# An attention and gated feed-forward kernel: a later value load, an output weight loaded in two parts, one half's attention placed earlier, and one more Strassen pair

## The chip, the core and the metric

The kernel runs on one core of one Trainium2 chip. The metric is the device time of one execution in microseconds (us). The kernel before takes 239.68 us, the median of three runs (239.47 to 240.16).

The engines are named as the profile names them: PE multiplies matrices (PEld loads its stationary operand), DVE works elementwise on tensors, ACT does activations and copies, POOL does simple elementwise work and issues some DMAs, SP issues DMAs. Each engine runs its own instructions in the order in which the program emits them.

## The reference

Four batches of eight heads, 768 positions, 64 channels a head. Each position attends to the 95 before it, itself, and eight global positions; a bias falls off linearly with distance. The result, as 3072 tokens of 512 channels, goes through a gated feed-forward with 1536 hidden channels:

```python
scores = scale * q @ k.T + bias            # kept where global or local, else -1e9
a = exp(scores - max); a = a / a.sum()
x = (a @ v), heads side by side            # 3072 x 512
out = (maximum(x @ w_gate, 0) * (x @ w_val)) @ w_out
```

## The kernel before, in words

The 3072 tokens are eight halves of 384, two to a batch, numbered 0 to 7 in the code; "the third half" is number 2. A half has three tiles of 128 tokens. Its work is: load q and k (`load_qk`, SP's queue) and v (`load_v_half`, POOL's queue); eight casts to bf16 on POOL (`piece_cast`); three DMA transposes on SP's queue (`piece_x`), which make queries and keys with the channels on partitions (tile `kqT`); copies that order the keys for the windows (`piece_order`, tile `kT`, two head pairs on POOL and, for the third half, two on ACT); attention of four pairs of heads; and the feed-forward.

Attention of a half is a list, `attention_pieces`: for each pair of heads three pieces `QK` (the scores in four PSUM banks, their exponentials on ACT, the masks on DVE), two pieces `AV` (the product with v on PE in one bank each, logarithm and inverse on ACT) and a norm `N` on DVE, which writes `xT`, the feed-forward's input. Scores and value products take turns in five banks `x`. Two gaps, of empty pieces, make up the list: with one piece in each it has 26 places, with two in each, as for the third half, 28.

The feed-forward of a half, `ffn_pieces`, is a list of pieces of four to eight matmuls, each with the weight 0.65: 24 that make gate and value for the twelve blocks of 128 hidden channels (`f1`: ReLU on ACT, product on DVE into tile `ht`), and then the output product (`f2`). A plain output tile is four pieces `outp` of three 512-column matmuls. A pair of tiles can instead go through Strassen's scheme (Winograd's form, `winograd`): seven products of six matmuls with 256 columns, four sums of hidden tiles (`add`, line 535, on DVE) and sums of the output weight (`wo_sum`, line 835, on DVE, made once). Each half multiplies its first two tiles this way, but for half 0; `PAIRED` names the halves whose third tile forms a pair with the next half's third tile (`sums3`, `add3`). Products of gate, value and output take turns in three banks `ff`, the Strassen products also in banks `x`.

The order of the work is written by hand. `weave` emits a list of feed-forward pieces one after the other and puts other pieces in between: an extra with position p is emitted as soon as the weights emitted so far reach p times the sum of the weights. `spread` gives a list of pieces evenly spaced positions. So PE's order is this order, and so is that of every engine for what is emitted through it. What is emitted outside runs at once as far as its engine and its data allow.

Around the change the order is this. Halves 0 and 1 have their attention at the start, the first weights arrive, and POOL issues the third groups of w_gate and w_val and then all of w_out (`wo_sb`, `loads`, line 798). POOL then fills the second v buffer with ones, issues the third half's v loads (line 841), makes seven casts, copies one element of `wo_sb` (tile `held`, line 845, which waits until w_out is there), and makes the eighth cast; SP issues the three transposes; POOL orders the keys of two pairs. Then `load_qk_after(3, nc.gpsimd)` lets POOL write one element of each staging tile, which stands ahead of SP's loads of the fourth half's q and k, and POOL issues that half's v. Three weaves follow; the third (lines 852 to 856) holds the last blocks of halves 0 and 1, their output products, the third half's attention and the fourth half's casts and transposes. The halves after that come from a loop (line 859).

Of the kernel before, what the change touches and what calls it, by code (L numbers as in the profile page):

```python
# [15 lines left out]
def kernel(  # L16
# [12 lines left out]
    nc = tc.nc  # L29
# [4 lines left out]
    DM = H * D  # L34
    DFF = moe_w_gate.shape[1]
    N_DC = DM // 128
    N_FC = DFF // 128
    HP = H // 2
    QH = S // 2
    NN = 3  # L40
# [55 lines left out]
    wo_sb = const.tile([128, N_FC, DM], BF16)  # L96
# [3 lines left out]
    def w_of(t, dc, fc):  # L100
        f = fc % GW
        return t[fc // GW][:, dc, f * 128 : (f + 1) * 128]
# [15 lines left out]
    def v_dst(b, r0, r1, j):  # L118
        t = vbuf[b % 2][r0:r1, j, D:]
        return t.rearrange("p (h z) -> p h z", z=2 * D)[:, :, 0:D]  # L120

    def load_v_globals(b):
        nc.gpsimd.dma_start(out=v_dst(b, 0, NG, 0),
                            in_=v[b, :, 0:NG, :].rearrange("h p d -> p h d"))

    def spread_v_globals(b, j0=1, j1=NT):
        if b == 0:
            for j in range(j0, j1):
                nc.sync.dma_start(out=v_dst(b, 0, NG, j), in_=v_dst(b, 0, NG, 0))
        else:  # L130
            t = vbuf[b % 2]
            nc.sync.dma_start(out=t[0:NG, j0:j1, :], in_=t[0:NG, 0:1, :].to_broadcast(
                [NG, j1 - j0, (2 * H + 1) * D]))

    def load_v(b, j, r0=0, r1=KT):
        n = min(r1, S - KT * j) - r0
        nc.gpsimd.dma_start(  # L137
            out=v_dst(b, NG + r0, NG + r0 + n, j),
            in_=v[b, :, KT * j + r0 : KT * j + r0 + n, :].rearrange("h p d -> p h d"))
# [5 lines left out]
    def load_v_half(s):  # L145
        b, half = divmod(s, 2)
        if half == 0:
            load_v_globals(b)
            if s != 2:
                spread_v_globals(b)  # L150
        for j in range(4) if half == 0 else range(4, NT):
            load_v(b, j)

    def load_w(dst, src, f0, f1):
        nc.gpsimd.dma_start(out=dst, in_=src[:, f0:f1].rearrange("(c p) f -> p c f", p=128))

    def load_w_group(i):
        load_w(wg[i], moe_w_gate, i * GW * 128, (i + 1) * GW * 128)
# [218 lines left out]
    def early_pieces(s):  # L377
        out = [(0.0, lambda p=p, i=i: piece_cast(s, p, i)) for i in range(2) for p in range(HP)]
        out += [(0.0, lambda n=n: piece_x(s, n)) for n in range(NN)]
        out += [(0.0, lambda p=p: piece_order(s, p)) for p in range(HP)]  # L380
        return out
# [111 lines left out]
    def attention_pieces(s):  # L493
        QK = lambda p: [(0.15, lambda g=g: piece_qk(s, p, g)) for g in range(3)]
        AV = lambda p: [(0.29, lambda e=e: piece_av(s, p, e)) for e in range(2)]
        N = lambda p: [(0.0, lambda: piece_norm(s, p))]
        g = QK(3)
        a = AV(2)
        gap = [(0.0, lambda: None)] * (2 if s == 2 else 1)
        return (QK(0) + QK(1) + AV(0) + N(0) + gap + QK(2) + AV(1) + N(1) + gap  # L500
                + g[0:1] + a[0:1] + g[1:2] + a[1:2] + g[2:3] + N(2) + AV(3) + N(3))

# [89 lines left out]
        return add, [(0.65, (m1, m2, m3, m4, m5, m6, m7)[i - 1]) for i in order]  # L592


    PAIRED = (4, 6)
    third_of = {}

    def ffn_pieces(c):
        ht = ht_pool.tile([128, N_FC, QH], BF16, name="ht")
        st = {}  # L600

        def product(w, key, fc, d0, d1):
            key = key, fc
            if d0 == 0 and key not in st:
                st[key] = psum["ff"].tile([128, 512], FP32, name="ff_ps")
            for dc in range(d0, d1):
                nc.tensor.matmul(st[key][:, 0:QH], lhsT=w_of(w, dc, fc), rhs=xT_of[c][:, dc, :],  # L607
                                 start=(dc == 0), stop=(dc == N_DC - 1))

        def gate(fc, d0=0):  # L610
            product(wg, "g", fc, d0, N_DC)
            psg = st["g", fc]
            gr = gr_pool.tile([128, QH], BF16, name="grelu")
            nc.scalar.activation(gr, psg[:, 0:QH], AF.Relu, bias=0.0, scale=1.0)  # L614
            st["gr", fc] = gr

        def val(fc, d0=0):
            product(wv, "v", fc, d0, N_DC)
            psv = st["v", fc]
            nc.vector.tensor_tensor(ht[:, fc, :], psv[:, 0:QH], st["gr", fc], op=ALU.mult)  # L620

        def outp(n, part):
            if part == 0:
                st["o"] = psum["ff"].tile([128, 512], FP32, name="ff_ps")
            ps2 = st["o"]
            for fc in range(part * N_FC // 4, (part + 1) * N_FC // 4):
                nc.tensor.matmul(ps2, lhsT=ht[:, fc, n * 128 : (n + 1) * 128],  # L627
                                 rhs=wo_sb[:, fc, :],
                                 start=(fc == 0), stop=(fc == N_FC - 1))
            if part == 3:  # L630
                osb = late["osb"].tile([128, DM], FP32, name="osb")
                nc.scalar.copy(osb, ps2)
                nc.sync.dma_start(out=out_v[c, n], in_=osb)

        def begin():
            two = psum["s"].tile([128, 2, 512], FP32, name="s_ps")
            st["g", 1], st["v", 1] = two[:, 0], two[:, 1]
            for d0, d1 in ((0, 2), (2, N_DC - 1)):
                for key, w in (("g", wg), ("v", wv)):
                    for fc in range(2):  # L640
                        product(w, key, fc, d0, d1)

        plain = range(NN) if c < 1 else () if c - c % 2 in PAIRED else (NN - 1,)
        add, products = winograd([(c, ht, 0), (c, ht, 1)], "sums", (1, 5, 6, 4, 7, 2, 3) if c == NHALF - 1 else
                                 (1, 2, 5, 6, 4, 3, 7) if c in PAIRED else (1, 5, 4, 6, 2, 3, 7))
        behind = {2: [lambda: add(3, 0, 3)], 7 if c == 2 else 5: [lambda: add(3, 3, 6)], 8: [lambda: add(1, 0, 3)],
                  9: [lambda: add(2, 0, 3)], 10: [lambda: add(4, 0, 3)]}
        rest = tuple(lambda j=j: add(j, 3, 6) for j in (1, 2, 4))
        if c in PAIRED:
            third_of[c] = ht  # L650
        elif c - 1 in PAIRED:
            add3, products3 = winograd([(c, ht, NN - 1), (c - 1, third_of[c - 1], NN - 1)], "sums3",
                                       (1, 5, 4, 6, 2, 3, 7))
            behind.update({1: [lambda: add3(1)], 6: [lambda: add3(2)], 7: [lambda: add3(3)]})
            rest = (lambda: add3(4),) + rest

        def val_and_sums(fc):
            val(fc)
            for f in behind.get(fc, ()):
                f()  # L660

        begin_of[c] = (begin, lambda fc=0: gate(fc, N_DC - 1), lambda fc=0: val(fc, N_DC - 1))
        f1 = []
        for fc in range(N_FC):
            f1.append((0.65, lambda fc=fc: gate(fc)))
            f1.append((0.65, lambda fc=fc: (val if c < 1 else val_and_sums)(fc)))
        f2 = [(0.65, lambda n=n, part=part: outp(n, part))
              for n in plain for part in range(4)]
        if c >= 1:
            f2 += (products3 if c - 1 in PAIRED else []) + products  # L670
            places = (2, 3, 5) if plain else (0, 1, 2) if c in PAIRED else (0, 1, 2, 3)
            for at, f in list(zip(places, rest))[::-1]:
                f2.insert(at, (0.0, f))
        return f1, f2


    def spread(items, first, last):

        n = len(items)
        return [(first + (i + 0.5) / n * (last - first), f) for i, (_, f) in enumerate(items)]  # L680
# [102 lines left out]
    f1_0, f2_0 = ffn_pieces(0)  # L783
# [13 lines left out]

    def loads():
        load_w_group(2)
        load_w(wo_sb, moe_w_out, 0, DM)  # L800
        Z()

    more = {"K0": lambda: load_qk_after(2), "S20": loads}
# [1 line left out]
    for f in ("m0 g0 g1 v0 m3 K3 m2 g2 m1 v1 K2 v2 S30 K0 S31 K1 S21 g3 S20 v3 S01 A3 N3 S00 S11 "  # L805
              "g6 g7 A2 S10 g4 v7 A0 N2 v4 v6 A1 N0 N1 g5 v5").split():
        i = int(f[1])
# [30 lines left out]
    nc.gpsimd.memset(vbuf[1][:, NT - 1, :].bitcast(mybir.dt.uint32), 0)  # L838
    for j in range(NT):
        fill_ones(nc.gpsimd, 1, j)  # L840
    load_v_half(2)
    E = [f for _, f in early_pieces(2)]
    casts, xs, order_k = E[0:8], E[8:11], E[11:15]
    held = rc_pool.tile([1, 1], BF16, name="held")
    for f in (*casts[:7], lambda: nc.gpsimd.tensor_copy(held, wo_sb[0:1, N_FC - 1, 0:1]),
              casts[7], *xs, lambda: spread_v_globals(1), *order_k[:2]):
        f()
    load_qk_after(3, nc.gpsimd)
    load_v_half(3)
    weave(f1_1[G[0]])  # L850
    weave(f1_1[G[1]], [(0.1 + 0.12 * j, lambda j=j: fill_ones(nc.vector, 0, j)) for j in range(NT)])
    weave(f1_0[G[2]] + f1_1[G[2]] + f2_0 + f2_1,
          [(0.33, order_k[2]), (0.38, order_k[3])],
          spread(attention_pieces(2), 0.375, 0.925), spread(early_pieces(3), 0.58, 0.88),
          spread([(0.0, lambda j=j, part=part: wo_sum(j, part)) for j in (1, 3, 2, 4) for part in range(2)],
                 0.1, 0.74))

    ahead = {}
    for c in range(2, NHALF):
# [53 lines left out]
```

## Time and profile before

| | us |
|---|---|
| median of three runs | 239.68 |
| lowest and highest | 239.47, 240.16 |
| the profiled execution | 240.08 |
| its span, first to last instruction | 238.3 |
| PE busy in the span | 231.7 |
| DVE, ACT, POOL busy | 171.8, 156.1, 89.5 |

The profile is of one execution. Its page gives busy times, the chain of work that ended last, and groups of equal instructions by line; the trace answers for stretches of time. A matmul's end is modelled and lies some 0.16 us past the start of the next one where they are dense, so PE's pace is read from start to start. TensorE's clock was granted in full from the first matmul to the last. The DMA engines move 132 GB/s in the mean; 47176 of 70515 packets are under 512 B. The third weave runs from about 46.3 to 76.2 us.

The page's lines on DMA issues (out<-in, issuing engine, count, KB each, median us from issue to landing) that bear on the change:

```profile
vbuf<-in_v_dram POOLq DMA_DIRECT2D x21, 120.0 KB, 7.7
wo_sb<-in_moe_w_out_dram POOLq DMA_DIRECT2D x1, 1536.0 KB, 19.0
```

### The profile page before, as it was taken

How to read it: one execution, taken by the hardware profiler on the slowest of the kernel's cores; microseconds unless marked ns; L12 is line 12 of the kernel's file. 1: busy time of each engine (PE TensorE's matmuls, PEld its weight loads, DVE VectorE, ACT ScalarE, POOL GpSimd, SP SyncE). 2: the span in 40 equal slices, each digit the busy share in tenths (PEclk: the TensorE clock that was granted, in tenths of full speed). 3: DMA queues.
4: the chain of work that ended last, by engine and by line, in shares of the span. 5: the costliest groups of instructions: out<-in, count | busy, mean ns of one | idle time of the engine just before them, and what ended most of it. 6: DMA issues, size and time to landing. Idle time of an engine off the chain costs nothing.

```text
span 238.3 us, 5431 instructions
## 1 busy us (share of the span) xinstructions
PE 231.7 (97%) x1977; PEld 150.1 (63%) x1981; DVE 171.8 (72%) x456; ACT 156.1 (66%) x358; POOL 89.5 (38%) x204
## 2 busy tenths in 40 slices
PE   7899999999999999999999999999999999999994
PEld 3655565655557566666667666856588666766683
DVE  7775965768756778666787677868985786955752
ACT  5896983438767777757777678557686578634330
POOL 6795897007433860903275042723350000000000
PEclk9999999999999999999999999999999999999999
DMA  6999999993996897098519955198432200020022
GB/s 208 183 170 174 241 263 213 191 162 47 286 205 124 260 194 135 10 183 259 101 33 111 236 155 111 25 157 249 78 59 88 90 1 0 4 88 0 3 80 97
DMA packets 70515, 31.42 MB, mean 132 GB/s; under 512 B 47176, under 2 KB 67400, under 8 KB 70488
## 3 DMA queue, kind: packets, MB, share of 16 engines
q0 software_dynamic: 32800, 8.71, 36.0%
q1 hardware_dynamic: 36472, 21.45, 34.3%
q10 hardware_dynamic: 1216, 0.92, 1.2%
q8 instruction: 15, 0.25, 0.4%
q14 instruction: 12, 0.10, 0.1%
HBM read 28.41 MB, written 6.29 MB: 146 GB/s over the span
## 4 chain that ended last, share of the span: by engine, by line
PE 86%; DMA 7%; DVE 2%; POOL 1%; ACT 1%; issue 1%; DVEq 0%
PE ff_ps L607 50%; PE ff_ps L549 12%; DMA wg<-in_moe_w_gate_dram 7%; PE ff_ps L627 7%; PE x_ps L427 6%; PE x_ps L549 5%; PE x_ps L397 4%; PE t_ps L700 1%; PE t_ps L459 1%; POOL kq L737 1%; PE t_ps L272 1%; DVE es L359 0%; DVE ht L620 0%; ACT lnd L436 0%; DVE osb L574 0%
## 5 line engine op out<-in xcount | busy, mean ns | idle before, releaser
L607 PE MATMUL ff_ps<-xT,wg 128*128 128x384 bf16 x380 | 77.7, 326 | 0.4 <-DMA wg<-in_moe_w_gate_dram 0.2
L607 PE MATMUL ff_ps<-xT,wv 128*128 128x384 bf16 x380 | 77.6, 326 | 0.2 <-DVE osb L574 0.2
L614 ACT ACTIVATE grelu<-ff_ps 128x384 bf16<-128x384 f32 x95 | 46.5, 491 | 45.1 <-PE ff_ps L607 23.2
L620 DVE TENSOR_TENSOR ht<-ff_ps,grelu 128x384 bf16<-128x384 f32 x95 | 52.7, 555 | 30.2 <-PE ff_ps L607 19.1
L607 PEld LDWEIGHTS <-wg 128*128 128x128 bf16 x384 | 36.1, 98 | 23.6 <-issue 1.0
L607 PEld LDWEIGHTS <-wv 128*128 128x128 bf16 x384 | 35.8, 98 | 23.3 <-issue 0.5
L406 ACT ACTIVATE es<-x_ps 128x360 bf16<-128x360 f32 (+2 forms) x96 | 35.6, 447 | 3.2 <-PE x_ps L397 3.2
L359 DVE TENSOR_TENSOR es<-es,m_all 128x432 bf16<-128x432 bf16 (+4 forms) x108 | 29.7, 325 | 6.0 <-ACT es L406 5.8
L446 DVE TENSOR_TENSOR xT<-x_ps,rcp 64x384 bf16<-64x384 f32 x48 | 26.6, 554 | 9.2 <-ACT rcp L441 8.4
L436 ACT ACTIVATE lnd<-x_ps 64x384 f32<-64x384 f32 x48 | 23.3, 485 | 10.9 <-PE x_ps L427 10.2
L363 POOL CAST kqc<-ks 128x384 bf16<-128x384 f32 x24 | 12.1, 554 | 31.7 <-DMA ks<-in_k_dram 31.7
L549 PEld LDWEIGHTS <-s 128*128 128x128 bf16 x216 | 21.1, 98 | 2.9 <-issue 0.4
L549 PE MATMUL ff_ps<-t,s 128*128 128x256 bf16 x162 | 21.6, 272 | 0.3 <-ACT osb L584 0.3
L427 PE MATMUL x_ps<-es,vbuf 128*128 128x216 bf16 (+4 forms) x216 | 21.8, 225 | 0.0
L137 POOL DMA_DIRECT2D vbuf<-in_v_dram x25 | 21.6, 881 | 0.3 <-DVE s L535 0.3
L427 PEld LDWEIGHTS <-vbuf 128*128 128x128 bf16 x216 | 15.8, 97 | 6.8
L627 PE MATMUL ff_ps<-wo_sb,ht 128*128 128x512 bf16 x68 | 17.6, 379 | 0.2
L549 PEld LDWEIGHTS <-ht 128*128 128x128 bf16 x162 | 15.5, 98 | 2.3
L263 POOL COPY kT<-kqT 128x240 bf16<-128x240 bf16 x16 | 7.1, 442 | 22.2 <-DMA kqT<-kqc 19.2
L363 POOL CAST kqc<-qs 128x384 bf16<-128x384 f32 x24 | 12.1, 541 | 6.2 <-DMA qs<-in_q_dram 6.2
L535 DVE TENSOR_TENSOR s<-ht 128x384 bf16<-128x384 bf16 (+1 forms) x32 | 12.5, 392 | 0.8
L441 ACT ACTIVATE rcp<-lnd 128x384 f32<-128x384 f32 x24 | 12.6, 524 | 0.8
(118 smaller groups left out, 247.0 us busy)
## 6 DMA issues: line engine op xcount, KB each, us to landing
out_dram<-osb SPq DMA_DIRECT2D x23, 256.0 KB, 2.4
ks<-in_k_dram SPq DMA_DIRECT2D x6, 768.0 KB, 6.2
qs<-in_q_dram SPq DMA_DIRECT2D x6, 768.0 KB, 11.5
vbuf<-in_v_dram POOLq DMA_DIRECT2D x21, 120.0 KB, 7.7
wo_sb<-in_moe_w_out_dram POOLq DMA_DIRECT2D x1, 1536.0 KB, 19.0
wg<-in_moe_w_gate_dram POOLq DMA_DIRECT2D x2, 512.0 KB, 9.8
wv<-in_moe_w_val_dram POOLq DMA_DIRECT2D x2, 512.0 KB, 11.0
wg<-in_moe_w_gate_dram POOLq DMA_DIRECT2D x2, 256.0 KB, 5.8
```

Of the source, the lines that this page charges most:

```text
L137: nc.gpsimd.dma_start(out=v_dst(b, NG + r0, NG + r0 + n, j), in_=v[b, :, KT * j + r0 : KT * j + r0 + n, :].rearrange("h p d -> p h d"))
L359: nc.vector.tensor_mul(for_all, for_all, mk)
L363: nc.gpsimd.tensor_copy(kqc[:, :, i].rearrange("t n (h d) -> t h n d", d=D)[:, 2 * p : 2 * p + 2], of[s][:, 2 * p : 2 * p + 2, :].rearrang ...
L406: nc.scalar.activation(es[:, e, 0:c], banks[e][:, 0:c], AF.Exp, bias=0.0, scale=scale)
L427: nc.tensor.matmul(av3[:, :, a : a + w], lhsT=vb[:, j, z0 : z0 + 128], rhs=es[:, e, c : c + NN * w].rearrange("k (n p) -> k n p", n=NN), s ...
L436: nc.scalar.activation(ln[o0 : o0 + 64], av[d0 : d0 + 64, 0:QH], AF.Ln, bias=0.0, scale=1.0)
L446: nc.vector.tensor_tensor(xT_of[s][r, p, :], av_of[s, p, e][r, 0:QH], av_of[s, p, "r"][r], op=ALU.mult)
L549: nc.tensor.matmul(st[key][:, 0:D2], lhsT=left(i), rhs=right(i), start=start and i == 0, stop=i == N2 - 1, skip_group_check=not start)
L607: nc.tensor.matmul(st[key][:, 0:QH], lhsT=w_of(w, dc, fc), rhs=xT_of[c][:, dc, :], start=(dc == 0), stop=(dc == N_DC - 1))
L614: nc.scalar.activation(gr, psg[:, 0:QH], AF.Relu, bias=0.0, scale=1.0)
L620: nc.vector.tensor_tensor(ht[:, fc, :], psv[:, 0:QH], st["gr", fc], op=ALU.mult)
L627: nc.tensor.matmul(ps2, lhsT=ht[:, fc, n * 128 : (n + 1) * 128], rhs=wo_sb[:, fc, :], start=(fc == 0), stop=(fc == N_FC - 1))
```

## The change

Four things are changed.

1. `PAIRED` becomes (0, 4, 6): the third tiles of halves 0 and 1 become a Strassen pair. Half 0 multiplies two tiles plainly, half 1 none. The pair's four sums stand between the pieces of half 0's plain tiles. For the later pairs, two of the four sums are made in two parts each, at more places (`behind`).
2. The third half's v loads are issued after its eight casts and three transposes. The `held` copy no longer stands before the eighth cast.
3. w_out is loaded in two parts, blocks 0 to 7 where it was loaded, and blocks 8 to 11 behind the key order of the third half's first two pairs. The `held` copy, which waits for the second part, comes behind that.
4. In the third weave, the third half's attention is spread over 0.18 to 0.88 instead of 0.375 to 0.925, with one gap at a time instead of two. ACT's key orders stand at 0.18 and 0.22 instead of 0.33 and 0.38, the sums of w_out at 0.34 to 0.63 instead of 0.1 to 0.74.

```diff
+    def load_wo(i0, i1):
+        nc.gpsimd.dma_start(out=wo_sb[:, i0:i1], in_=moe_w_out[i0 * 128 : i1 * 128].rearrange("(c p) f -> p c f", p=128))
...
-        gap = [(0.0, lambda: None)] * (2 if s == 2 else 1)
+        gap = [(0.0, lambda: None)]
...
-    PAIRED = (4, 6)
+    PAIRED = (0, 4, 6)
...
-        plain = range(NN) if c < 1 else () if c - c % 2 in PAIRED else (NN - 1,)
+        plain = range(2) if c < 1 else () if c - c % 2 in PAIRED else (NN - 1,)
...
-            behind.update({1: [lambda: add3(1)], 6: [lambda: add3(2)], 7: [lambda: add3(3)]})
-            rest = (lambda: add3(4),) + rest
+            if c > 1:
+                behind[1] = [lambda: add3(1)]
+                for fc, j, i in ((3, 2, 0), (4, 3, 0), (6, 2, 3), (7, 3, 3)):
+                    behind[fc] = [lambda j=j, i=i: add3(j, i, i + 3)]
+                rest = (lambda: add3(4),) + rest
+            else:
+                for j in range(1, 5):
+                    f2_0.insert(2 * j - 1, (0.0, lambda j=j: add3(j)))
...
-            places = (2, 3, 5) if plain else (0, 1, 2) if c in PAIRED else (0, 1, 2, 3)
+            places = (2, 3, 5) if plain else (0, 1, 2) if c in PAIRED or c == 1 else (0, 1, 2, 3)
...
-        load_w(wo_sb, moe_w_out, 0, DM)
+        load_wo(0, 8)
...
-    load_v_half(2)
...
-    for f in (*casts[:7], lambda: nc.gpsimd.tensor_copy(held, wo_sb[0:1, N_FC - 1, 0:1]),
-              casts[7], *xs, lambda: spread_v_globals(1), *order_k[:2]):
+    for f in (*casts, *xs, lambda: load_v_half(2), lambda: spread_v_globals(1), *order_k[:2],
+              lambda: load_wo(8, N_FC), lambda: nc.gpsimd.tensor_copy(held, wo_sb[0:1, N_FC - 1, 0:1])):
...
-          [(0.33, order_k[2]), (0.38, order_k[3])],
-          spread(attention_pieces(2), 0.375, 0.925), spread(early_pieces(3), 0.58, 0.88),
+          [(0.18, order_k[2]), (0.22, order_k[3])],
+          spread(attention_pieces(2), 0.18, 0.88), spread(early_pieces(3), 0.58, 0.88),
...
-                 0.1, 0.74))
+                 0.34, 0.63))
```

More of the change, by code (lines that the diff above doesn't have):

```diff
@@ L641, in begin @@
                         product(w, key, fc, d0, d1)
-        plain = range(NN) if c < 1 else () if c - c % 2 in PAIRED else (NN - 1,)
+        plain = range(2) if c < 1 else () if c - c % 2 in PAIRED else (NN - 1,)
         add, products = winograd([(c, ht, 0), (c, ht, 1)], "sums", (1, 5, 6, 4, 7, 2, 3) if c == NHALF - 1 else
-                                 (1, 2, 5, 6, 4, 3, 7) if c in PAIRED else (1, 5, 4, 6, 2, 3, 7))
+                                 (1, 2, 5, 6, 4, 3, 7) if c in PAIRED else (1, 5, 4, 6, 2, 3, 7)) if c else ((), ())
         behind = {2: [lambda: add(3, 0, 3)], 7 if c == 2 else 5: [lambda: add(3, 3, 6)], 8: [lambda: add(1, 0, 3)],
```

## Prediction

> **What bounds the kernel now.** I read the page first, then the chain of waits in order of time, then the timelines of PE, POOL and SP around the third half's queries and keys, then busy time by stretch. The page, its span and its busy shares:
>
> ```profile
> span 238.3 us, 5431 instructions
> ...
> PE 231.7 (97%) x1977; PEld 150.1 (63%) x1981; DVE 171.8 (72%) x456; ACT 156.1 (66%) x358; POOL 89.5 (38%) x204
> ...
> PE 86%; DMA 7%; DVE 2%; POOL 1%; ACT 1%; issue 1%; DVEq 0%
> ```
>
> PE sets the time: 86% of the chain is PE, and the 7% of DMA is the wait for the first weights, before 27.7 us, which the change does not touch. So an edit is worth the PE time it removes, or a stall of PE that it removes or makes. Modelled ends of matmuls run past the next start, so I count from start to start. From 34.5 us on PE stops visibly in three places only. The chain in order of time shows them (start, us, what):
>
> ```profile
> 61.58 1.94 PE ff_ps L627 x9
> ...
> 74.77 0.53 ACT rcp L441
> ...
> 75.91 0.56 DVE xT L446
> 76.50 0.42 DVE osb L569
> 76.92 0.34 DVE osb L574
> 77.31 1.47 PE ff_ps L607 x8
> ...
> 169.74 0.48 DVE ht L620
> 170.26 2.11 PE ff_ps L607 x12
> ...
> 225.57 1.31 PE ff_ps L549 x12
> ```
>
> Stops one and two come at the end of the stage in which the third half's attention is woven (call it G2): its last logarithms and inverse hold ACT, so a Strassen copy comes late (product 7 starts at 75.60, its predecessor's six matmuls of 0.109 were through at 75.18: 0.42 us); its last norms hold DVE at 75.33 to 76.47, so a sum frees its bank late (77.31 where 76.25 + 4 x 0.1636 = 76.90: 0.41 us). The third, 0.34 us before 170.26, is in the sixth half: DVE is late with a product of gate and value. Rows 61.58 and 225.57 give the price of a matmul: 1.94/9 = 0.2157 us for 512 columns, 1.31/12 = 0.1093 us for 256.
>
> **The work itself.** Two third tiles as plain products were 24 matmuls of 512 columns, 24 x 0.2157 = 5.18 us. As a pair they are 7 x 6 = 42 of 256, 42 x 0.1093 = 4.59 us. **-0.6 us.** The evacuation changes from two ACT copies of 580 ns to four of 370 ns, plus four DVE operations of 420 ns and four sums (L535, 128x768) of 546 to 627 ns: 4 us more on DVE, where it hides only if DVE has room (below).
>
> **The stalls removed.** The third half's 26 attention pieces now end at 0.88 of 38 items instead of 0.925 of 39 (an item is one piece of the weave, 0.65 in its own unit, 0.655 us on PE): last norm behind item 33, 5 items ahead of the end instead of 3. ACT and DVE are then through before the last products. I count both stops as gone: **-0.8 us**. Halving the third-tile sums of halves six and eight takes 0.3 us of DVE (0.71 at 167.52 becomes about 0.37) from in front of the late multiply: **-0.3 us**. It reappears two pieces earlier, in DVE gaps of 0.8 and 0.4 us. Sum of the gains: 1.7 us.
>
> **What comes forward.** The first scores of the third half ran at 56.76, behind item 16. At 0.1935 x 38 = 7.4 they now come behind item 8: 56.76 - 8 x 0.655 = 51.52 us. What they need is in the timelines of POOL and of SP (start, us, what, in brackets the idle time before it and what ended it):
>
> ```profile
> 40.10 1.53 POOL L363 CAST kqc<-qs 128x384 bf16<-128x384 f32 x3 [1.56 <-DMA qs<-in_q_dram]
> 47.47 0.18 POOL L845 COPY held<-wo_sb 1x1 bf16<-1x1 bf16 x1 [5.83 <-DMA wo_sb<-in_moe_w_out_dram]
> ...
> 54.92 0.63 POOL L259 COPY kT<-kqT 128x360 bf16<-128x360 bf16 x1 [6.83 <-DMA kqT<-kqc]
> ```
>
> SP's issue of the three transposes, merged into one line:
>
> ```profile
> 48.12 4.84 SPq L368 DMA_TRANSPOSE kqT<-kqc  x3
> ```
>
> The query load ends the first wait at 40.10, and nothing moves it. Without the one-element copy that waits for wo, the eighth cast ends at 40.10 + 4 x 0.5 = 42.1, and SP can issue the transposes at 42.15 instead of 48.12. From issue to POOL's first copy took 6.8 us there (54.92), 5.9 us at 89.46 where nothing else was in flight (95.38). Now two transfers are in flight beside them: the rest of wo's first part (1 MB; at the 208 GB/s of 42 to 44.8 us it ends near 44.9 instead of 47.4) and the V loads, which POOL now issues at 42.2 to 46.5. At best the transposes are in at 42.15 + 5.9 = 48.1; 4 us of that are their 0.79 MB at 191 GB/s (91 to 94 us). If they shared evenly, they would give up as much time as the others use meanwhile: 1.5 us of wo (43.4 to 44.9) and some 2.4 of the V loads' 3.4 us (0.49 MB at the 146 GB/s of 48 to 49.3 us), 52.0. I take 50.4, between the two, because POOL's transfers begin late beside SP's (page: 7.7 us to landing; 4.4 at 99 to 105 us, where no SP load is in flight), so the first half of the transposes meets wo alone. POOL then orders the keys of the first pair in 1.0 to 1.3 us (L259 to L261), ready at 51.4 to 51.8. **+0.3 us** of stall; 0 if transposes land by 50.2, 1.8 if at 52.0.
>
> The Trainium skill (DMA: Bandwidth & Descriptors, section on queues, rings and completion order) says that each DMA engine round-robins between the queue rows it has work for. By that rule the even sharing, 52.0, would hold from the start; the 7.7 against 4.4 us says only that a POOL transfer suffers, not that SP's does not. It is the rival below.
>
> V: last issue at 45.6 + 7.7 = 53.3, the first value product (behind item 14) is at about 56.5. The SP copy of the global rows stands behind the transposes as before. Hidden.
>
> **ACT beside the first scores.** The two key orders on ACT (0.72 us each, 55.30 and 56.60) were at 0.33 and 0.38, where ACT had only ReLUs. At 0.18 and 0.22 the second one stands between the exponentials of the first pair's two groups. ACT: ReLU to 53.2, order to 53.9, exponentials of group two, first one out at 54.3. The second pair's scores (behind item 11, 53.96) want five x banks' third reuse: their last group takes the bank that this exponential frees. PE there at 54.1. **+0.2 us** (0 to 0.5).
>
> **DVE behind it.** From item 16 (58.5) to item 24 DVE now has: norms of the first pair (58 + 56, ready when ACT's inverse is, 59.2 to 60.4), five sums of wo (0.55 each, 0.47 apart), the four new third-tile sums (0.5 apart), masks of the third pair (0.92 in all), then the second pair's norms. 2.4 + 2.0 + 0.9 = 5.3 us: the first of these norms ends at 60.4 + 5.3 + 0.55 = 66.2. It frees the x bank for which the fourth pair's scores, behind item 25, stand at 65.6. **+0.6 us** (0 to 1.1: the one-item gap ahead of these scores is all the cover there is). In the stretch 86 to 96 us, DVE was busy 8.74 of 10 us without a stall, so a full DVE alone is not a stall; this one is late by order.
>
> **wo's second part and the fourth half's loads.** POOL issues the second part behind the ordering (53.0). 512 KB: 4.4 us for a V tile alone, less its 0.85 us, plus 2.5 at 208 GB/s = 6 us, landing 59.0. PE first reads it in the third piece of the plain tiles, past 61; DVE past 60.4. Hidden, with 2 us. The copy that waits for it holds POOL, so the fourth half's query and key loads (memset at 57.39) start near 59.2, 1.8 later. Before, from that memset to its first keys ordered were 18.9 us (76.27), used at 78.71; now 78.1, used at 78.2 to 78.5 by my sum. No term, but no cover left: a later landing is paid by PE one for one.
>
> **Sum.** 240.08 (span 238.3) - 1.7 + 0.3 + 0.2 + 0.6 = 239.5. The profiled execution stands 0.40 above the median of the three runs, so **239.1 us** against 239.68. A measurement here tells about 0.3% from no change, 0.72 us: faster is under 238.96, slower over 240.40.
>
> **Rivals.** (B) The new waits are small: transposes by 50.2, DVE in time for the banks. Then 0 to 0.6 of the 1.1 is paid: 238.0 to 238.9. For it: no row shows a bank wait of this kind in the halves that run at the same density (86 to 96 us). Against: none of those carries eight sums of wo. (C) Slower: the DMA engines share evenly and the transposes land at 52.0 or later. It decides at the first scores: from 51.1 on, with the other two waits, nothing of the gain is left, and from 51.8 on the change is slower by over 0.3%. Price at 52.0: 1.8 instead of 0.3, 240.6; at 52.6, 241.2. For it: DMA share 1.24 and 2.20 of 16 engines in those stretches, no room. (D) The second part of wo queues (9.8 us, as the page's 512 KB loads did, instead of 6): all of the fourth half's chain is 1 to 3 us late, and PE waits at the third scores of the next half: 240 to 242. Against: those loads stood behind others in POOL's queue. That the change does not do what it says, I leave out: each piece can be followed in the code.
>
> **Chances.** Forecast (238.7 to 240.0) 0.45, B 0.30, C 0.15, D 0.10. Faster: most of B and a quarter of the forecast, 0.40; slower: C's and D's larger part, 0.18; same 0.42. Range 238.1 to 240.8: it leaves out the best of B and the worst of C and D. The forecast's own range is 238.7 to 240.0.
>
> **What would show it.** Matmuls of L627: 24 fewer; of L549: 42 more. The chain without ACT and DVE at the end of G2 and at 170. POOL's first key copy at about 50.4 (C: 52 or more). PE idle ahead of the first third-half scores, released by POOL, 0.3; ahead of the fourth pair's scores, released by a DVE norm, 0.6. POOL's held copy near 59 (D: 63) and PE dense at the next half's first scores. I am wrong if PE waits in G2 for something else, wo or a Strassen sum above all.

## The result, and the profile after

The changed kernel takes 249.24 us in the median of six runs (245.63 to 251.46) against 239.78 us (239.47 to 240.16) for the kernel before beside it: the ratio is 1.030, 95% interval 1.024 to 1.036. It is slower, and outside the forecast's range. Ratios here and below leave out runs over 1.5% above the fastest run of their kernel; the ratio of the two medians is 1.039. The profiled execution took 246.71 us, near the lower end of its runs. Lines after the diff's first hunk stand three higher than before (L607 is now L610, L397 L400, L446 L449), those of the last part ten or eleven.

The page of the kernel after, its span, busy shares, chain by engine and one group; the group's last columns are busy time and mean ns, then the idle time before it and what ended most of that:

```profile
span 244.9 us, 5480 instructions
...
PE 233.1 (95%) x1996; PEld 152.3 (62%) x1999; DVE 176.3 (72%) x468; ACT 156.7 (64%) x360; POOL 90.9 (37%) x205
...
PE 74%; DMA 8%; DVE 7%; issue 4%; POOL 2%; ACT 2%; SPq 1%; POOLq 0%; DVEq 0%
...
L400 PE MATMUL x_ps<-kqT,kT 64*128 64x216 bf16 (+4 forms) x216 | 11.6, 227 | 6.0 <-POOL kT L264 5.4
```

PE has fallen from 86 to 74 per cent of the chain; PE now stood for 6 us ahead of scores, nearly all of it released by POOL's key copies. The chain of waits in order of time (start, us, what) names what stood behind the copies:

```profile
46.65 9.07 DMA kqT<-kqc
...
55.87 0.54 POOL kT L262
...
56.77 0.69 PE x_ps L400 x6
57.46 3.66 PE ff_ps L610 x12
...
73.14 0.31 PE x_ps L400 x2
...
81.89 1.31 PE ff_ps L552 x12
83.19 0.81 PE ff_ps L610 x5
```

The third transpose, issued at 46.65, holds the chain for 9.07 us. Behind the first scores stand twelve matmuls of 384 columns in 3.66 us, 0.305 us each where such a matmul costs 0.164 elsewhere. At the end of G2 nothing but PE is on the chain any more: the two stops there are gone, and the last products run straight into the next half. The timelines of POOL and SP answer to those shown of before:

```profile
41.93 1.86 POOL L366 CAST kqc<-qs 128x384 bf16<-128x384 f32 x4 [5.73 <-DMA qs<-in_q_dram]
...
44.33 3.62 POOL L137 DMA_DIRECT2D vbuf<-in_v_dram  x4
55.87 0.54 POOL L262 COPY kT<-kqT 128x360 bf16<-128x360 bf16 x1 [7.92 <-DMA kqT<-kqc]
```

```profile
43.82 4.87 SPq L371 DMA_TRANSPOSE kqT<-kqc  x3
```

The transposes are issued 4.3 us earlier than before (43.82 for 48.12), and POOL's first copy comes 0.95 us later than before (55.87 for 54.92). The waits of PE from 45 to 84 us (line, releaser: us in total, times, longest):

```profile
PE x_ps L400 <- POOL kT L264: 5.4, 1, 5.4
PE x_ps L400 <- DVE xT L449: 0.6, 1, 0.6
```

From start to start the first wait lost 5.55 us (51.06 to 56.77), the second 0.72. Busy times by stretch show what the first left behind (after the engines come the granted clock, DMA share, GB/s):

```profile
53.00:57.00 4.00, 0.23 (x4) 0.20 (x6) 0.00 (x0) 0.81 (x3) 1.13 (x4) 0.61 0.96 101
57.50:61.00 3.50, 3.50 (x12) 1.53 (x11) 1.20 (x4) 2.25 (x8) 0.81 (x2) 0.54 0.35 33
```

PE is full from 57.5 to 61 us, but at a granted clock of 0.54: after the long stop the next 3.5 us of matmuls run at half rate. **The sum of the loss** is counted from start to start and behind both stops of before: the second group of four matmuls of the next half begins at 83.68 instead of 77.31, 6.37 us later. 5.55 for the first scores, 12 x (0.305 - 0.164) = 1.7 for the slow matmuls and 0.7 for the fourth pair's scores, less the 0.6 and 0.8 that the prediction gained in this stage, are 6.55; 0.2 is not told apart. From there to the end it is 161.2 us, 0.2 more than before (161.0). The stop in the sixth half is still there, 0.24 us where it was 0.34 (the four matmuls from 175.98 are through at 176.63):

```profile
175.98 0.81 PE L610 MATMUL ff_ps<-xT,wv 128*128 128x384 bf16 x4
176.87 0.81 PE L610 MATMUL ff_ps<-xT,wg 128*128 128x384 bf16 x4
```

### The profile page after: what moved, and what is told of

Same layout as the page of the kernel before. It is cut to its first block, busy times and chain, and to the rows that moved or that the text cites. A ratio compares the mean times of both kernels' runs of the same rounds, so it can differ in the third digit from the quotient of the medians.

```text
span 244.9 us, 5480 instructions
## 1 busy us (share of the span) xinstructions
PE 233.1 (95%) x1996; PEld 152.3 (62%) x1999; DVE 176.3 (72%) x468; ACT 156.7 (64%) x360; POOL 90.9 (37%) x205
## 4 chain that ended last, share of the span: by engine, by line
PE 74%; DMA 8%; DVE 7%; issue 4%; POOL 2%; ACT 2%; SPq 1%; POOLq 0%; DVEq 0%
PE ff_ps L610 40%; PE ff_ps L552 13%; PE x_ps L552 5%; PE x_ps L430 5%; DMA kqT<-kqc 4%; PE x_ps L400 4%; DMA ks<-in_k_dram 2%; PE ff_ps L630 2%; DVE s L538 2%; DVE ht L623 2%; POOL kqc L366 1%; DMA kq<-in_k_dram 1%; DVE t L845 1%; PE t_ps L275 1%; DVE es L362 1%
## 5 line engine op out<-in xcount | busy, mean ns | idle before, releaser
L610 PE MATMUL ff_ps<-xT,wg 128*128 128x384 bf16 x380 | 78.7, 329 | 0.1
L610 PE MATMUL ff_ps<-xT,wv 128*128 128x384 bf16 x380 | 78.3, 329 | 0.0
L610 PEld LDWEIGHTS <-wg 128*128 128x128 bf16 x384 | 36.3, 98 | 24.1 <-issue 2.4
L610 PEld LDWEIGHTS <-wv 128*128 128x128 bf16 x384 | 35.8, 98 | 23.4 <-issue 0.7
L362 DVE TENSOR_TENSOR es<-es,m_all 128x432 bf16<-128x432 bf16 (+4 forms) x108 | 30.3, 332 | 9.6 <-ACT es L409 9.6
L449 DVE TENSOR_TENSOR xT<-x_ps,rcp 64x384 bf16<-64x384 f32 x48 | 26.6, 554 | 5.0 <-ACT rcp L444 4.3
L366 POOL CAST kqc<-ks 128x384 bf16<-128x384 f32 x24 | 14.1, 630 | 30.1 <-DMA ks<-in_k_dram 28.0
L552 PEld LDWEIGHTS <-s 128*128 128x128 bf16 x240 | 23.3, 98 | 2.8
L552 PE MATMUL ff_ps<-t,s 128*128 128x256 bf16 x180 | 24.1, 273 | 0.0
L552 PEld LDWEIGHTS <-ht 128*128 128x128 bf16 x180 | 17.2, 98 | 2.7
L400 PE MATMUL x_ps<-kqT,kT 64*128 64x216 bf16 (+4 forms) x216 | 11.6, 227 | 6.0 <-POOL kT L264 5.4
L538 DVE TENSOR_TENSOR s<-ht 128x384 bf16<-128x384 bf16 (+1 forms) x36 | 14.8, 412 | 0.8
L400 PEld LDWEIGHTS <-kT 64*128 64x128 bf16 x216 | 6.1, 95 | 13.7 <-issue 6.6
```

What stands on the lines that cost most here:

```text
L362: nc.vector.tensor_mul(for_all, for_all, mk)
L366: nc.gpsimd.tensor_copy(kqc[:, :, i].rearrange("t n (h d) -> t h n d", d=D)[:, 2 * p : 2 * p + 2], of[s][:, 2 * p : 2 * p + 2, :].rearrang ...
L400: nc.tensor.matmul(banks[e][:, c : c + NN * w].rearrange("k (n t) -> k n t", n=NN), lhsT=kt[r, j, :], rhs=qd[r, :, a : a + w], start=True, ...
L449: nc.vector.tensor_tensor(xT_of[s][r, p, :], av_of[s, p, e][r, 0:QH], av_of[s, p, "r"][r], op=ALU.mult)
L552: nc.tensor.matmul(st[key][:, 0:D2], lhsT=left(i), rhs=right(i), start=start and i == 0, stop=i == N2 - 1, skip_group_check=not start)
```

## The experiments

Ratios are to the kernel before, run beside each. "Theory A" is that V's packets beside the transposes are the loss.

**The pair.** e1_pair_alone is the kernel before with the pair and the halved sums only:

```diff
-    PAIRED = (4, 6)
+    PAIRED = (0, 4, 6)
...
-                 0.1, 0.74))
+                 0.1, 0.63))
```

> The kernel before with only the new pair (third tiles of halves 0 and 1) and the halved third-tile sums; loads, key order and attention stay where they were, and the sums of w_out end at 0.63 instead of 0.74 so that the pair can read them. Theory A (the loss comes from the transposes of the third half's queries and keys, slowed by the V loads beside them): nothing of it is here, so the gain of the products and of the later halves stays: 238.3 to 239.4 us. Rival B (the pair's extra DVE work jams the stage): 240 us or more, with PE waiting for DVE between 57 and 76 us.

Measured: 241.0 us, ratio 1.005 (1.003 to 1.007). The pair alone already loses. The two largest waits of PE from 45 to 85 us:

```profile
PE x_ps L397 <- DVE xT L446: 0.7, 2, 0.4
PE ff_ps L607 <- DVE osb L574: 0.5, 1, 0.5
```

DVE is busy 11.81 of 13.5 us from 56.5 to 70 (9.68 before): norms come late for the banks that scores want, and a Strassen sum is late at the end of G2. e9_pair_attention_to_088 took that last stop away with attention at 0.385 to 0.88 and one gap:

> e1_pair_alone with the attention of the third half at 0.385 to 0.88 and one gap, as dense as in the other halves. If the stops of e1_pair_alone before the fourth half (0.6 us, the last norms late) come from attention ending late, they go and the time is 240.0 to 240.6; if the jam of DVE between 57 and 70 us (waits of 0.2 to 0.6 us for norms) only grows with the density, 241 or more.

Measured: 240.67 us, 1.003 (1.001 to 1.005), the end stop gone. e11_pair_sums_of_wo_earlier took more of DVE's collisions away:

```diff
-                 0.1, 0.63))
+                 0.04, 0.42))
```

> The kernel before with the third-tile pair, the halved sums and the third half's attention ending at 88 per cent (240.67 us), and the eight sums of wo spread over 4 to 42 per cent of the weave in place of 10 to 63, where VectorE stands idle from 48 to 51 us in that run's trace. Theory N (the pair alone loses because the norms reach VectorE behind sums): the 0.54 us stop before the fourth pair's scores goes and the whole is 239.4 to 240.2 us, level with the kernel before. Rival: the sums wait for wo at 48.1 and hold gates behind them, and the whole is 240.5 to 241.5.

Measured: 239.87 us, 1.0003 (0.9985 to 1.002): level with before, and the stop at 63 fell from 0.54 to 0.26 (it stands ahead of the third pair's scores; the expectation's "fourth" is a slip). With the sums of w_out out of their way the pair and the halved sums cost what they gain; of the stops left between 55 and 73 us the longest are 0.59, 0.53 and 0.25, and which of them eats the gain is not shown. e13_attention_at_0405 moved the attention to 0.405 to 0.89:

> The version level with the kernel before (239.87 us: pair, halved sums, sums of wo over 4 to 42 per cent), with the third half's attention at 40.5 to 89 per cent in place of 38.5 to 88. Theory N (what is left of the pair's loss are short waits at the edges of the attention): the first scores come 0.6 us later and no longer wait (0.59 us), and the whole is 239.2 to 239.7 us. Rival: the norms and masks, pressed together by as much, make the stops of 0.26, 0.23 and 0.54 us longer, and the whole is 239.8 to 240.5 us.

Measured: 239.92 us, 1.0003 (0.999 to 1.0015). The rival held: the first scores no longer wait, and a stop of 0.69 came at 67.5. No version here beat the kernel before.

**The transposes and V.** e2_without_pair is the change with `PAIRED = (4, 6)`:

> The changed kernel with the new pair undone (plain third tiles again in halves 0 and 1), all moves of loads and attention kept. Theory A: the first key copy on POOL still comes near 56 us and PE still stops for some 5 us ahead of the first scores: 246 to 251 us. Rival B: DVE relieved, 243 us or less.

Measured: 247.67 us, 1.029 (1.023 to 1.034); the first scores still lose 5.6 us. The pair is not the loss. e3_v_behind_key_order issues V behind POOL's key copies:

```diff
-    for f in (*casts, *xs, lambda: load_v_half(2), lambda: spread_v_globals(1), *order_k[:2],
+    for f in (*casts, *xs, *order_k[:2], lambda: load_v_half(2), lambda: spread_v_globals(1),
```

> The changed kernel with one move: the third half's V loads are issued behind the key order of the first two pairs, so that no V packet is in flight beside the transposes. Theory A: key copies on POOL begin 6 to 7 us after the transposes' issue, near 50.5 us; the 5.5 us stop and the slow clock behind it are gone. V is then issued at 53 to 57 and lands 58 to 61, so the first value products wait 1 to 4 us: 240 to 243.5 us. Rival C (the transposes are slow for another reason, the rest of w_out or the place in the program): the first key copy stays at 54 us or later, 247 us or more.

Measured: 246.79 us, 1.027 (1.021 to 1.032). SP's and POOL's lines and the longest wait of PE in e3:

```profile
43.09 4.11 SPq L371 DMA_TRANSPOSE kqT<-kqc  x3
...
50.95 0.54 POOL L262 COPY kT<-kqT 128x360 bf16<-128x360 bf16 x1 [7.89 <-DMA kqT<-kqc]
```

```profile
PE x_ps L430 <- DMA vbuf<-in_v_dram: 5.9, 1, 5.9
```

Issued at 43.09, the transposes are in at 50.95, 7.9 us, where with V beside them it takes 12.0; the first scores lose 0.67. Theory A holds for the transposes. But V lands at 63.0 and the first value product waits 5.9 us, more than I expected: the same transfer time is paid at another place.

e4_attention_where_it_was puts attention back to 0.375 to 0.925 and ACT's key orders to 0.33 and 0.38:

> The changed kernel with the third half's attention and the two key orders on ACT back at 0.375 to 0.925, 0.33 and 0.38; loads as changed. Theory A: the key copies stay near 56 us, but the scores are due at 56 too, so that stop shrinks to under 1 us. The second part of w_out is issued behind the key copies, lands near 63.5, and the plain tiles are due for it at about 60: PE waits 3 to 4 us there, 242.5 to 244.5 us. Rival D (the late w_out has cover): 239 to 240.5 us.

Measured: 247.18 us, 1.030 (1.025 to 1.034), worse than expected. Its two longest waits of PE:

```profile
PE ff_ps L630 <- DMA wo_sb<-in_moe_w_out_dram: 3.5, 1, 3.5
PE x_ps L400 <- DVE xT L449: 1.6, 2, 1.3
```

With no early attention in front of them the plain tiles stand for wo's second part, which lands at 63.7 because it is issued behind the late key copies. So moving the attention back saves nothing: the late transposes cost through wo instead.

**V ahead of everything.** e5_v_before_w_out puts `load_v_half(2)` in front of `load_wo(0, 8)`; e6_v_first_small_w_out does so with `load_wo(0, 6)` and the rest later.

> The changed kernel with the third half's V loads issued ahead of w_out's first part (they are in by about 43 us), so that only w_out's rest is in flight beside the transposes. Theory A in its form 'the two queues take turns packet by packet': w_out now ends some 3.4 us later, near 48.8, and its 1 KB packets hold each turn longer than V's 128 B ones, so the key copies begin at 52.5 to 54, PE stops 2 to 3 us ahead of the first scores, 241.5 to 244 us. Form 'V's small packets are what hurts': copies at 50 to 51.5, stop under 1.3 us, 239.5 to 240.8 us. Rival C (neither, the place in the program): 55 us or later, 246 or more.

> As e5_v_before_w_out, and the first part of w_out is blocks 0 to 5 only (the second part 6 to 11), so that it ends 1.3 us earlier, near 47. Turn by turn: copies at 51 to 52.5, stop 0.8 to 2 us; the second part, 768 KB, is issued near 54 and lands near 61, where the plain tiles are due for it: 239.5 to 243 us. Small packets alone: as e5_v_before_w_out, 239.3 to 240.8.

Measured: 245.2 us, 1.020 (1.016 to 1.024), and 245.38 us, 1.023 (1.018 to 1.027). Neither tested Theory A: I left POOL's fill of the same buffer behind the loads, so it waited for them to land (6.2 us in e6), and the casts and the issue of the transposes (48.48, 47.95) came late. Alone, these took 6.5 and 6.3 us. e7_fill_v_then_w_out mends that, and takes the fill and the loads away from where they stood:

```diff
         load_w_group(2)
+        nc.gpsimd.memset(vbuf[1][:, NT - 1, :].bitcast(mybir.dt.uint32), 0)
+        for j in range(NT):
+            fill_ones(nc.gpsimd, 1, j)
+        load_v_half(2)
         load_wo(0, 8)
...
```

> The change, with V's border fill and then V's five loads ahead of the first part of wo on POOL's queue (in the run before of this kind the fill stood behind V's loads and waited for them, which put the casts back by 4 us). Theory A (V's packets beside the transposes are the loss): V has landed by 43.6 us, the casts end by 43.9, the transposes run beside the rest of wo's first part alone and land at 51 to 52.5; the stop before the first scores is 0 to 1.6 us, no slow matmuls behind it, and the whole is 239 to 242 us. Rival S (anything beside the transposes slows them as much as V does): they land at 55 to 56, the stop stays 4 to 5 us and the whole is 245 to 249.

Measured: 243.9 us, 1.016 (1.013 to 1.018), between the two. SP's and POOL's lines in e7:

```profile
42.80 7.31 SPq L371 DMA_TRANSPOSE kqT<-kqc  x3
...
53.98 0.54 POOL L262 COPY kT<-kqT 128x360 bf16<-128x360 bf16 x1 [11.20 <-DMA kqT<-kqc]
```

V is in at 43.9, the transposes are issued at 42.80, and the first copy comes at 53.98, 11.2 us later. Now wo's first part, landing at 49.6, stands in V's place: no transpose packet moves before 46.1, and only some 270 per us until 49 (685 to 823 in e3's full microseconds). So Theory A was too narrow and rival S too: V costs more, but wo's first part beside the transposes costs 3 us as well. e12_v_first_attention_at_032 is e7 with attention at 0.32:

> V's fill and loads ahead of the first part of wo (243.9 us), and the third half's attention at 32 to 88 per cent of the weave in place of 18, so that the first scores come at some 55.5 us, behind the key copies at 54 to 55.6. Theory A (what the change loses is the wait of the first scores and its slow matmuls, and nothing else of size): both go, 3.3 and 1.1 us, and the whole is 239.3 to 241 us if nothing else turns up. Rival W (the attention that was moved forward also covered the second part of wo): with the attention later the plain tiles come up sooner, at about 60 us, and wait for that part, which lands at about 61.9; the stop is 1 to 2.5 us, and the whole is 241 to 243 us.

Measured: 242.59 us, 1.012 (1.010 to 1.014): W's range, but only partly W's reason. The clock stays at 1.000 and the first scores lose nothing. A direct wait for wo costs 0.4 us, a Strassen product that waits for a sum of wo 1.3, norms 0.5 and 0.6, and 1.7 us go at 52.64 to ACT:

```profile
53.27 0.55 ACT L262 COPY kT<-kqT 128x360 bf16<-128x360 bf16 x1 [2.37 <-DMA kqT<-kqc]
```

I had left ACT's key copies at 0.18. They wait for the transposes there, and a ReLU, for which a bank of PE stands, is queued behind them.

**The slow matmuls, and what spreads the runs.** e8_dummy_matmuls_in_the_stop adds 25 matmuls of 512 columns, results unused, ahead of the first scores:

```diff
-          [(0.18, order_k[2]), (0.22, order_k[3])],
+          [(0.18, order_k[2]), (0.22, order_k[3])], [(0.19, warm)],
...
```

> The changed kernel with 25 matmuls of 512 columns, whose result nothing reads, ahead of the third half's first scores (25 x 0.2157 = 5.4 us, about the length of the stop). If the slow matmuls behind the stop (0.32 instead of 0.164 us, 11 of them, 1.8 us) come from PE's idleness, they are gone and the time falls by 1 to 2 us, to 245.5 to 248 median with granted clock near 1.0; if they come from anything else, 249 us as the changed kernel.

Measured: 248.99 us, 1.033 (1.027 to 1.039). No slow matmuls stand behind the first scores, and the mean clock of its four runs is 0.991 to 0.998 (0.979 to 0.993 in the six of the kernel after), so the idle time had caused them. But nothing was won. In the profiled execution (249.14 us) the key copies begin at 52.89, while the added matmuls hold PE until 57.26; and a new stop of 3.17 us stands ahead of the fourth pair's scores, with half-rate matmuls behind it. DVE there in e8, then in the kernel after, and POOL in e8:

```profile
66.70 0.86 DVE L538 TENSOR_TENSOR s<-ht 128x768 bf16<-128x768 bf16 x1
67.49 0.85 DVE L845 TENSOR_TENSOR t<-wo_sb 128x768 bf16<-128x768 bf16 x1
68.26 0.85 DVE L538 TENSOR_TENSOR s<-s,ht 128x768 bf16<-128x768 bf16 x1
...
73.91 1.14 DVE L449 TENSOR_TENSOR xT<-x_ps,rcp 64x384 bf16<-64x384 f32 x2
```

```profile
67.78 0.55 DVE L538 TENSOR_TENSOR s<-ht 128x768 bf16<-128x768 bf16 x1
68.25 0.55 DVE L845 TENSOR_TENSOR t<-wo_sb 128x768 bf16<-128x768 bf16 x1
68.72 0.55 DVE L538 TENSOR_TENSOR s<-s,ht 128x768 bf16<-128x768 bf16 x1
```

```profile
66.52 2.95 POOL L366 CAST kqc<-ks 128x384 bf16<-128x384 f32 x4 [3.13 <-DMA ks<-in_k_dram]
```

The sums start every 0.78 us in e8 and every 0.47 in after. In e8 POOL's casts of the fourth half run between them; in after the first cast comes up at 69.65 and takes 3.22 us, since DVE leaves it no gap. e5's profile (250.47 us) has the same stop of 3.2 us. The Trainium skill (SBUF — State Buffer, section on the two separate sides) says that DVE, with two inputs from SBUF, and POOL take one pair of ports in turns, the first to start holding it for its whole instruction. The rows agree: 0.31 us lost per sum while POOL casts.

e10_sixth_casts_left_out leaves out seven of the eight casts in `early_pieces(3)`, so those keys and queries are stale. (Label and expectation call it the sixth half; it is the fourth, number 3.)

> The change, with seven of the eight casts of the sixth half's keys and queries (POOL, 66 to 77 us) left out: the transposes of that half then move stale data, so its output rows are not the reference's; every wait around them stays. The first stop (5.5 us before the first scores, with the slow matmuls behind it) is untouched. Theory J: what parts the runs of the changed kernel at 246 us from those at 249 to 251 us is a second long stop, about 3 us before the fourth pair's scores with slow matmuls of its own, and it comes where POOL's casts fall between VectorE's 768-wide sums, which then start every 0.77 us in place of 0.47: with the casts gone no run has it, all lie between 244.5 and 247 us, the mean clock of each is 0.985 or more, and the profile shows the sums every 0.47 us throughout. Rival K: the second stop comes from the late second part of wo and the number of sums alone, with POOL innocent: runs at 249 to 251 us at a clock near 0.979 remain among ten.

Measured: 248.96 us, 1.033 (1.028 to 1.037), runs from 246.0 to 251.11. Theory J fell as the cause of the spread. In the profiled execution (250.22 us) the sums do start every 0.47 us and the stop is 0.73, as J says of that place, though the profile of the kernel after shows both with the casts in. Rival K's sign came, runs at 249 to 251 us with a clock of 0.979, but not its second stop. In this execution the query load landed at 43.98 and the transposes at 58.94, the first scores lost 7.66 us, and 1.7 us were lost to weights before 32 us. In the kernels with the changed order of loads the query load lands between 38.4 and 44.0, and with V beside the transposes the first key copy follows it, at 52.9 to 58.9. In the five profiles with the old order (before, e1, e9, e11, e13) the query load lands between 38.8 and 42.5 as well, and the first copy lies within 54.6 and 55.1, because the wait for wo stands over it. That this wider landing, with DVE's jam behind it, makes up the whole spread of 245.6 to 251.5 us is argued, not shown: the kernel after has one profile.

## Why the prediction was wrong

The step that failed is the one in "What comes forward": "I take 50.4, between the two, because POOL's transfers begin late beside SP's", with its **+0.3 us**. It was 55.87 and 5.55 us, and 1.7 more that the sum had no term for.

- **The issue.** Taken as 42.15, it was 43.82: the query load landed at 41.88, not 40.05. "Nothing moves it" was wrong; it lands 5.6 us apart in profiles whose loads up to there are the same (38.4 in e8, 44.0 in e10). 1.7 us of the error.
- **Issue to first copy.** Taken as 8.25 us, 5.9 alone and 2.35 for sharing, it was 12.05. 3.8 us of the error. The 5.9 was short: e3, with none of V and only 6 packets of wo beside the transposes, took 7.9, of which 2.2 lie behind its last transpose packet (0.6 in before, e5 and e6). Sharing with V came to 4.2 on top of e3.
- **When V began.** That V begins late held for the first of the three transposes only. Its 1024 packets passed from 45.09 to 46.55 beside 64 packets of V (the 8 KB load), since V's first large load begins at 46.61. The other two took from 47.30 to 54.86, 7.6 us, with some 3360 packets of V among them; in e3 they took 2.9.
- **How they shared.** From 48 to 50 us, 378 and 441 packets of POOL's queue passed per us beside 377 and 413 of the transposes. The two queues of the kernel after in these 2 us (q1 is SP's, q0 POOL's; packets, MB, share of 16 engines):

```profile
q1 hardware_dynamic: 790, 0.20, 79.4%
q0 software_dynamic: 819, 0.10, 76.3%
```

  These counts agree with the rule quoted from the Trainium skill (DMA: Bandwidth & Descriptors, section on queues, rings and completion order), turns between the queue rows; how many pieces of 128 or 256 bytes make one turn the trace does not show. Even sharing was rival C, with 0.15: right in kind, but priced at 52.0 with 2.4 us for V. I divided bytes by rates (146 GB/s): V has 0.49 MB to the transposes' 0.79, but 3904 packets to their 3072. A stand-still of about 1 us falls into the stretch too (last section); how the 4.2 us divide between it and V's turns is not shown.
- **The price of a wait.** I counted a wait as its own length. The stop of 5.5 us also cost 1.7 us of half-rate matmuls.
- **What held.** Both stops at the end of G2 went. The fourth pair's scores took 0.72 for 0.6, by the DVE norm as said. Ahead of the second pair's scores there is no stop, so the 0.2 for ACT was not paid. The matmul counts fit (19 more on the page, 18 expected). V, POOL's copies and wo's second part moved with the late transposes: the held copy ran at 63.72 for "near 59", but no wait of the next half followed, so D did not come.
- **What did not come.** The 0.3 of the later halves: 0.2 us was lost there, and the third stop stayed, in this execution. In e1, e4 to e8, e11 and e12 the same stretch takes 160.6 to 160.7 us and that stop is gone, so the term can be had; why it stays in after, e2, e3 and e9 is not shown.
- **What e1 adds.** The pair's 0.6 was not free even without the rest: by 0.5% the pair loses, through DVE. The prediction saw the late norm, but called the pair's gains and this wait separate terms; alone the pair shows two more waits of that kind.

## What to carry to other kernels

A wait that is taken away may have been keeping two transfers apart: before moving a load, count the packets, and not the bytes alone, that will be in flight beside the transfer on the critical path. A wait can also absorb the spread of a load behind it, so its removal makes the time follow that spread. Price a stop of PE of over 3 us with the slow matmuls behind it: nine of the ten such stops in these profiles had them.

## What the runs showed of the hardware

- Small packets of two queues passed nearly one for one while a transpose and V both moved (790 and 819 from 48 to 50 us in after). From the transposes' issue to the first copy it took 12.0 to 12.9 us with V beside them (after, e2, e4, e8, e10), 6.3 to 7.9 with none of V (e3, e5, e6) or only its last 370 packets (before).
- About 1 us in the middle of the transposes nearly everything stands: in after the trace shows 9 to 18 GB/s from 52.1 to 53.1 us with the engines fully busy, packets of both queues taking up to 1.66 us. It begins behind one 16 KB packet on the instruction queue (51.16); e2 and e4 show the same at 51.4 and 50.6. Whether that packet causes it is open.
- Behind the stop of 5.5 us the granted clock is 0.54 in the mean from 57.5 to 61 us. The length of a stop does not settle it alone: the clock fell to 0.50 for 3.4 us, 1.1 us after stops of 3.3 us in e7 and 3.2 us in e8, but stayed at 1.00 behind a stop of 3.7 us in e4. The stretches behind the stop in e7 and in e4 (granted clock third from the end):

```profile
55.98:59.39 3.41, 3.41 (x18) 1.39 (x17) 1.79 (x6) 2.66 (x9) 0.79 (x1) 0.50 0.43 60
```

```profile
63.80:67.20 3.40, 3.40 (x23) 1.67 (x22) 3.40 (x10) 2.08 (x4) 3.02 (x6) 1.00 0.34 81
```
